# Retention scores in four 64x64 tiles with an AND mask, and shorter groups of constant matmuls in the first tile

## The chip, the cores and the metric

The kernel runs on one core of one Trainium2 chip. The metric is the time of one execution on the device in microseconds (us), the median of several runs. Beside the timed runs stands one profiled execution, from which all rows of the trace come.

## The reference

Three layers follow each other: a retention layer over q, k, v, a two-matrix MLP with a normalization ahead of it, and a mixture of four attention experts. The change touches the first alone:

```python
B, H, S, D = 2, 8, 768, 64
gamma = 1.0 - 2.0 ** (-5.0 - np.arange(H))
for t in range(S):
    state = gamma * state + einsum('bhd,bhe->bhde', k[:, :, t], v[:, :, t])
    y[:, :, t] = scale * einsum('bhd,bhde->bhe', q[:, :, t], state)
...
xn = (x - mu) / sqrt(var + 1e-06) * g_ln
x = x + maximum(xn @ w_ch1, 0.0) @ w_ch2
```

Written over chunks of tokens, a token's result is the sum of a product with the state of the chunks before and of masked scores inside its own chunk: a key counts only where it is not later than the query.

## The kernel before, in words

The retention runs over 12 tiles, (batch, chunk of 128 tokens), in `r_tile`. For one tile and the 8 heads, in pairs p of two heads h:

- the scaled values `vs` come from POOL (L422), from the load of `vk` and a small table;
- PE makes the scores (L432): for each pair and head one float32 matmul of 64 rows (the head's 64 dimensions) by 128 keys over 128 queries, into the PSUM banks `PA[0]` and `PA[1]`. The two heads of a pair lie in the two halves of the partitions, so two matmuls can run side by side;
- DVE multiplies the scores with the mask `caus` of ones and zeros into `AM` (L438);
- PE adds, in PSUM, the product with the state (L451, "inter") and the masked scores with the values (L460), and updates the state from keys and values (L467);
- the result is scaled (L476), transposed on PE (L483), normalized, transposed again and split into a rounded part and a remainder, which the MLP's matmuls (L589, L608) read.

In the trace each of these float32 matmuls is two instructions, so the 8 matmuls of a tile's scores are 16 rows' worth; transpositions are one each.

The first lines of the program issue loads on SP's queue in the order kq of tile 0 in two halves (with `tabV` and `caus` behind the first), vk, tabY, ident, then the next tiles. While the first loads are on their way, PE runs matmuls of a constant tile `negs` (`spin`, L389): 4 ahead of the scores of the first half, 2 between the halves, 8 behind the second half. The value matmuls of the first tile stand behind the last of them by the key `"spun"`:

```python
spin(4, 2.0, [], ["spun"])
...
spin(*((2, 0.5), (8, 1.7))[y0], ["scored"], ["spun"])
...
PE(1.0, intra, r=[vs] + AM + (y if c else []) + (["spun"] if i == 0 else []), w=y)
```

What stands in which order on an engine is decided by a planner (`Plan`): each step carries its engine and a cost in us (the first number in `PE(1.3 / ny, ...)`, `DVE(0.69, ...)`), its reads and its writes; `issue` plays the steps through in time by these costs and takes, whenever an engine is free, the step of lowest priority number that can run. So another cost of one step can give another order of all steps behind it, on all engines. The program's order is then fixed; what waits on the chip is held by semaphores.

Of the kernel before, what the change touches and what calls it, by code (L numbers as in the profile page):

```python
# [24 lines left out]
F32 = mybir.dt.float32  # L25
# [3 lines left out]
OP = mybir.AluOpType  # L29
# [3 lines left out]
B, H, S, D = 2, 8, 768, 64  # L33
DM = H * D
FF = 4 * DM
E, HD = 4, 64
C = 128
NC = S // C
# [14 lines left out]
KB = 256  # L53
# [154 lines left out]
def region(base, size, n, space="S"):  # L208
    return [(space, base + i * size, size) for i in range(n)]
# [3 lines left out]
def retention_channel_mlp_mixture_attention(ctx: ExitStack, tc: tile.TileContext, a):  # L213
    nc = tc.nc
    pe, act, dve, pool, sp = nc.tensor, nc.scalar, nc.vector, nc.gpsimd, nc.sync
# [3 lines left out]
    cst = ctx.enter_context(tc.tile_pool(name="cst", bufs=1))  # L219
    pp = ctx.enter_context(tc.tile_pool(name="pp", bufs=1, space=PSUM))  # L220
    ident = cst.tile([128, C], F32, name="ident")
    caus = cst.tile([128, C], F32, name="caus")
    tabV = cst.tile([128, NC, H], F32, name="tabV")
    gln = cst.tile([128, NK], F32, name="gln")
    half = cst.tile([128, 1], F32, name="half")
# [3 lines left out]
    ps = pp.tile([128, 8 * 512], F32, name="ps")  # L229
# [19 lines left out]
    def typed(dt):  # L249
        def get(b, n=None):  # L250
            v = view(b)
            if v.dtype != dt:
                v = v.bitcast(dt)
            return v[:, :n] if n else v
        return get

    f32, f32r, u32 = typed(F32), typed(F32R), typed(U32)

    o_r = 0
    o_raw = o_r + 60 * KB  # L260
# [8 lines left out]
    x = o_r  # L269
    PL = {}  # L270
    for n, size, cnt in (("kq", 4, 4), ("vk", 4, 3), ("vs", 2, 2), ("am", 2, 4), ("sn", 1, 4), ("tabY", 2, 2),
                         ("xn", 2, 2), ("xc", 2, 2)):
        PL[n] = region(x, size * KB, cnt)
        x += size * cnt * KB
    assert x <= o_raw
    PL["raw"] = region(o_raw, 4 * KB, 3)
    PL["wy"] = region(o_raw + 16 * KB, 2 * KB, 2)
    PL["wx"] = region(o_raw + 20 * KB, 2 * KB, 1)
# [12 lines left out]
    x = o_h - 2 * (4 * KB + 16)  # L291
# [22 lines left out]
    def new(n):  # L314
        return Buf(PL[n], n)

    def PE(c, fn, r=(), w=(), hold=()):
        P.add({"T": c}, lambda e: fn(), r, w, lat=0.2, hold=hold)
# [4 lines left out]
    def DVE(c, fn, r=(), w=()):  # L323
        P.add({"V": c}, lambda e: fn(), r, w)
# [4 lines left out]
    def DMA(nbytes, fn, r=(), w=()):  # L329
        P.add({"D": nbytes / 320e3 + 0.05}, lambda e: fn(), r, w, lat=2.2)  # L330
# [33 lines left out]
    def r4(ap):  # L364
        return ap.rearrange("p (a t) -> p a t", a=4)

    def load(i):
        b, c = tiles[i]
        kq, vk = new("kq"), new("vk")
        n = 2 if i == 0 else 1  # L370
        for y in range(n):
            h = slice(1024 // n * y, 1024 // n * (y + 1))
            DMA(512e3 / n, lambda h=h: sp.dma_start(f32(kq)[:, h], a["kq"][b, c][:, h]), w=[(kq, y)])
            if i == 0 and y == 0:
                DMA(24e3, lambda: sp.dma_start(tabV, a["tabV"]), w=["tabV"])
                DMA(64e3, lambda: sp.dma_start(caus, a["caus"]), w=["caus"])
        DMA(512e3, lambda: sp.dma_start(f32(vk), a["vk"][b, c]), w=[vk])
        if b == 0:
            ty = TY[c] = new("tabY")
            DMA(256e3, lambda: sp.dma_start(f32(ty), a["tabY"][c]), w=[ty])  # L380
        L[i] = (kq, vk)

    DVE(0.2, lambda: dve.memset(negs, NEG), w=["negs"])
    IDLE = new("ps")

    def spin(n, c, r, w):
        def mm():
            for _ in range(n):
                pe.matmul(f32(IDLE)[:, :C], lhsT=negs, rhs=negs, start=True, stop=True)  # L389
        PE(c, mm, r=["negs"] + r, w=[IDLE] + w)  # L390

    spin(4, 2.0, [], ["spun"])
    load(0)
    DMA(64e3, lambda: sp.dma_start(ident, a["ident"]), w=["ident"])
    load(1)
    load(2)
    DMA(2e3, lambda: sp.dma_start(gln, a["gln"]), w=["gln"])
    DVE(0.1, lambda: dve.memset(half, -0.5), w=["half"])
# [15 lines left out]
    def r_tile(i):  # L414
        b, c = tiles[i]
        j, cc = divmod(c, TPB)
        kq, vk = L[i]
        pair = lambda z, p: f32(kq)[:, p // 2 * 512 + z * 256 + p % 2 * C:p // 2 * 512 + z * 256 + (p % 2 + 1) * C]
# [5 lines left out]
             r=[vk, "tabV"], w=[vs])  # L424
        PA, AM = [new("ps") for _ in range(2)], [new("am") for _ in range(2)]
        ny = 2 if i == 0 else 1
        for y0 in range(ny):
            def scores(y0=y0):
                for p in range(4 // ny * y0, 4 // ny * (y0 + 1)):
                    for h in range(2):  # L430
                        hs = slice(64 * h, 64 * h + 64)
                        pe.matmul(f32(PA[h])[:, p * C:(p + 1) * C], lhsT=pair(0, p)[hs], rhs=pair(1, p)[hs],  # L432
                                  start=True, stop=True)
            PE(1.3 / ny, scores, r=[(kq, y0)] + (["spun"] if i == 0 else []), w=PA + (["scored"] if i == 0 else []), hold=AM)
            if i == 0:
                spin(*((2, 0.5), (8, 1.7))[y0], ["scored"], ["spun"])
        for h in range(2):
            DVE(0.69, lambda h=h: dve.tensor_tensor(r4(f32(AM[h])), r4(f32(PA[h])),  # L438
                                                    caus[:, None, :].to_broadcast([128, 4, C]), OP.mult),
                r=[PA[h], "caus"], w=[AM[h]])  # L440
        st = SN.get(b)
        y = [new("ps") for _ in range(2)]
        place = lambda g, w, z: f32(y[w])[64 * g:64 * g + 64, z * C:(z + 1) * C]
# [37 lines left out]
        def tr(dst, src):  # L481
# [3 lines left out]
           r=[(xt, cc, 0), (xt, cc, 1), "ident"], w=[t1])  # L485
# [8 lines left out]
        def rstd():  # L494
# [5 lines left out]
            r=[t1, (mv, 1)], w=[xn])  # L500
# [462 lines left out]
    for i in range(NTI):  # L963
        if i + 3 < NTI:
            load(i + 3)
        for n in early.get(i, ()):
            load_piece(*pieces[n])
        r_tile(i)
        for n in early.get(i, ()):
            P.bias += 40  # L970
            split_piece(*pieces[n])
            P.bias -= 40
# [12 lines left out]
    for n, (f, b, j) in enumerate(steps):  # L985
# [16 lines left out]
        elif j == 1:  # L1002
            hs = m_h7(f, b, rest)
# [37 lines left out]
def _layouts(q, k, v, moe_g_ln, moe_w_ch1, moe_w_ch2, moe2_w_gate, moe2_wq, moe2_wk, moe2_wv, moe2_wo):  # L1041
    def chunks_t(x):
        return x.reshape(B, NP // 2, 2, 2, NC, C, D).transpose(0, 4, 3, 6, 1, 2, 5).reshape(B, NC, 128, NP // 2, 2 * C)

    def tokens(x):
        return x.reshape(B, H, NC, C, D).transpose(0, 2, 3, 1, 4).reshape(B, NC, C, DM)

    def kxn(w):
        return w.reshape(w.shape[0] // 128, 128, w.shape[1]).transpose(1, 0, 2)

    def experts(w):
        return w.transpose(1, 0, 2).reshape(DM, E * HD)

    def f64_bits(w):
        return np.ascontiguousarray(w).reshape(NFC, 128, 1024).view(np.int64)

    order = np.arange(DM).reshape(2, 2, 2, D).transpose(2, 0, 1, 3).reshape(DM)
    moe_g_ln, moe_w_ch1, moe_w_ch2 = moe_g_ln[order], moe_w_ch1[order], moe_w_ch2[:, order]
    moe2_w_gate, moe2_wq, moe2_wk, moe2_wv = moe2_w_gate[order], moe2_wq[:, order], moe2_wk[:, order], moe2_wv[:, order]
    gamma = 1.0 - 2.0 ** (-5.0 - np.arange(H, dtype=np.float64))  # L1060
    t = np.arange(S, dtype=np.float64)
    up = gamma[:, None] ** -(t + 1)
    down = gamma[:, None] ** (t + 1) / math.sqrt(D)
    r = np.arange(C)
    o = {
        "kq": np.stack([chunks_t(k), chunks_t(q)], axis=4).reshape(B, NC, 128, 2 * DM),
        "vk": np.stack([tokens(v), tokens(k)], axis=3).reshape(B, NC, C, 2 * DM),
        "tabV": up.reshape(H, NC, C).transpose(2, 1, 0).astype(np.float32),
        "tabY": np.repeat(down, D, axis=0)[order].reshape(NP, 128, NC, C).transpose(2, 1, 0, 3).reshape(NC, 128, NP * C).astype(np.float32),
        "caus": (r[:, None] <= r[None, :]).astype(np.float32),  # L1070
        "future": (r[:, None] < r[None, :]).astype(np.uint32),
        "ident": np.eye(C, dtype=np.float32),
        "before": np.broadcast_to(np.arange(E)[None, :] < np.arange(E)[:, None], (128, E, E)).astype(np.float32),
        "gln": moe_g_ln.reshape(NK, 128).T,
        "w1": f64_bits(moe_w_ch1.reshape(NK, 128, NFC, FC).transpose(2, 1, 0, 3)),
        "w2": f64_bits(moe_w_ch2.reshape(NFC, FC // 128, 128, DM).transpose(0, 2, 1, 3)),
        "wq": kxn(experts(moe2_wq)), "wk": kxn(experts(moe2_wk)),
        "wv": kxn(np.concatenate([experts(moe2_wv), moe2_w_gate], axis=1)),
        "wo": kxn(moe2_wo.reshape(E * HD, DM)),
    }  # L1080
    return {n: np.ascontiguousarray(x) for n, x in o.items()}
# [16 lines left out]
```

## Time and profile before

| | us |
|---|---|
| median of 3 runs | 453.73 (453.58 to 453.96) |
| the profiled execution | 454.83 |
| its span, first to last instruction | 453.0 |
| busy: PE, DVE, ACT, POOL | 444.2, 326.8, 224.2, 209.6 |

The profiled execution took 454.83, of which the trace shows a span of 453.0; 1.83 lie around it. Busy time of PE counts overlapping matmuls once. Where rows are merged, "x16" is 16 instructions; a start and a length of a merged row let the time from one group's start to the next be read. The retention stage fills the first 65 us, with the MLP's first matmuls in between.

### The profile page before, as it was taken

What the parts mean: (1) busy time and instruction counts of PE and PEld (TensorE: products, weight loads), DVE (VectorE), ACT (ScalarE), POOL (GpSimd) and SP (SyncE); (2) the same over time, 40 slices, a digit from 0 to 9 for tenths busy, and PEclk for the clock granted to TensorE, in tenths of its full rate; (3) what the DMA queues carried; (4) which work ended last, traced back from release to release, by engine and by line L of the source; (5) the groups of instructions that cost most, each with busy time, mean ns of one, the idle gap of its engine ahead of it and who ended that gap; (6) DMA issues with size and microseconds to landing.
All of it is one profiled execution on the core that took longest, in us unless ns stands there. A gap on an engine that the chain in (4) does not pass through costs nothing.

```text
span 453.0 us, 8497 instructions
## 1 busy us (share of the span) xinstructions
PE 444.2 (98%) x3214; PEld 417.8 (92%) x3214; DVE 326.8 (72%) x707; ACT 224.2 (49%) x469; POOL 209.6 (46%) x216
## 2 busy tenths in 40 slices
PE   8999999999999999999999999999999999999996
PEld 7778889999999999999999999999999887898775
DVE  1798786868759867876868665569558878788852
ACT  1377567164346436344354164235535666546852
POOL 1588768978989415326145064100401334133530
PEclk9999999999999999999999999999999999999999
DMA  7798924204103103113021002002231221101111
GB/s 266 283 373 311 352 69 140 94 1 140 46 1 130 56 1 117 71 46 137 5 86 55 1 1 93 2 0 95 69 72 27 63 52 47 48 1 46 49 48 46
DMA packets 14985, 40.11 MB, mean 89 GB/s; under 512 B 2272, under 2 KB 4960, under 8 KB 14944
## 3 DMA queue, kind: packets, MB, share of 16 engines
q1 hardware_dynamic: 14944, 39.57, 25.7%
q8 instruction: 25, 0.41, 0.3%
q14 instruction: 16, 0.13, 0.1%
HBM read 33.27 MB, written 3.15 MB: 80 GB/s over the span
## 4 chain that ended last, share of the span: by engine, by line
PE 86%; DVE 8%; ACT 2%; issue 2%; DMA 1%; POOL 0%; DVEq 0%; ACTq 0%
PE ps L608 28%; PE ps L669 19%; PE ps L589 7%; PE ps L753 7%; PE ps L790 4%; PE ps L917 3%; PE ps L902 3%; PE ps L941 3%; PE ps L432 2%; PE ps L483 2%; PE ps L460 2%; PE ps L860 2%; DVE sm L868 1%; PE ps L861 1%; PE ps L389 1%
## 5 line engine op out<-in xcount | busy, mean ns | idle before, releaser
L608 PE MATMUL ps<-h,w 128*128 128x384 f32 x768 | 145.6, 335 | 0.7 <-DVE xT L612 0.4
L608 PEld LDWEIGHTS ps<-h,w 128*128 128x128 f32 x768 | 134.0, 188 | 1.4 <-DVE xT L612 0.7
L612 DVE TENSOR_TENSOR xT<-xT,ps 128x384 f32<-128x384 f32 x112 | 60.2, 549 | 36.9 <-PE ps L608 36.6
L882 POOL TENSOR_SCALAR pr<-pr,sm,gate 128x384 f32<-128x384 f32 (+5 forms) x48 | 35.1, 744 | 81.7 <-DVE ps L867 28.8
L545 POOL TENSOR_TENSOR w<-wy,w 128x512 fp32r<-128x512 f32 x26 | 33.6, 1299 | 44.2 <-PE ps L608 39.7
L669 PE MATMUL ps<-t,S 128*128 128x384 f32 x216 | 43.1, 334 | 0.0
L870 ACT ACTIVATE pr<-ps,sm 128x384 f32<-128x384 f32 (+5 forms) x48 | 30.4, 635 | 18.8 <-DVE sm L868 12.3
L676 ACT ACTIVATE u<-ps 128x384 f32<-128x384 f32 x36 | 17.6, 490 | 41.4 <-PE ps L669 35.7
L669 PEld LDWEIGHTS ps<-t,S 128*128 128x128 f32 x216 | 37.9, 188 | 0.1
L589 PE MATMUL ps<-x,w 128*128 128x384 f32 x192 | 34.9, 336 | 0.4 <-ACT wx L520 0.4
L520 ACT ACTIVATE wx<-raw 128x512 f32<-128x512 f32 x32 | 21.6, 673 | 27.5 <-DVE ps L524 19.7
L589 PEld LDWEIGHTS ps<-x,w 128*128 128x128 f32 x192 | 33.2, 188 | 0.8 <-ACT wx L520 0.6
L868 DVE TENSOR_REDUCE sm<-ps 128x1 f32<-128x384 f32 (+5 forms) x48 | 30.0, 624 | 2.8
L521 POOL TENSOR_SCALAR wx<-wx 128x512 f32<-128x512 f32 x32 | 20.3, 634 | 18.5 <-ACT wx L520 17.7
L669 PE MATMUL ps<-x,w 128*128 128x384 f32 x144 | 28.8, 334 | 0.0
L684 ACT ACTIVATE h<-ps 128x384 fp32r<-128x384 f32 x36 | 17.6, 490 | 22.5 <-PE ps L608 14.4
L669 PEld LDWEIGHTS ps<-x,w 128*128 128x128 f32 x144 | 25.3, 188 | 0.0
L544 ACT ACTIVATE w<-wy 128x512 fp32r<-128x512 f32 x26 | 16.3, 628 | 16.4 <-PE ps L608 16.1
L522 DVE TENSOR_SCALAR ps<-wx 128x512 uint32<-128x512 uint32 x32 | 22.0, 686 | 2.2 <-POOL wx L521 1.8
L526 DVE SCALAR_TENSOR_TENSOR wy<-raw,ps 128x512 uint32<-128x512 uint32 x32 | 21.8, 682 | 1.9 <-POOL w L545 1.3
L902 PE MATMUL ps<-ident,pr 128*128 128x128 f32 x168 | 22.5, 276 | 0.6 <-ACT ob L334 0.4
L524 DVE SCALAR_TENSOR_TENSOR ps<-wx,ps 128x512 uint32<-128x512 uint32 x32 | 22.3, 696 | 1.1
(119 smaller groups left out, 883.6 us busy)
## 6 DMA issues: line engine op xcount, KB each, us to landing
raw<-in_w_dram SPq DMA_DIRECT2D x32, 512.0 KB, 3.5
vk<-in_vk_dram SPq DMA_DIRECT2D x12, 512.0 KB, 5.8
kq<-in_kq_dram SPq DMA_DIRECT2D x11, 512.0 KB, 5.4
qk<-qk SPq DMA_DIRECT2D x32, 96.0 KB, 2.1
out_dram<-ob SPq DMA_DIRECT2D x11, 256.0 KB, 2.0
tabY<-in_tabY_dram SPq DMA_DIRECT2D x6, 256.0 KB, 5.2
vraw<-in_wv_dram SPq DMA_DIRECT2D x1, 520.0 KB, 3.5
kq<-in_kq_dram SPq DMA_DIRECT2D x2, 256.0 KB, 2.9
```

The lines of the kernel that those rows point to most:

```text
L522: DVE(0.62, lambda: dve.tensor_scalar(u32(z), u32(x), 4, 1, op0=OP.logical_shift_left, op1=OP.logical_shift_right), r=[x], w=[z])
L524: DVE(0.7, lambda: dve.scalar_tensor_tensor(u32(z), u32(x), 0x80000000, u32(z), op0=OP.bitwise_and, op1=OP.bitwise_or), r=[x, z], w=[z])
L545: POOL(1.34, lambda: pool.tensor_tensor(f32r(l), f32(y), f32(h), OP.subtract), r=[y, h], w=[l])
L589: pe.matmul(f32(pa, TB), lhsT=wt, rhs=blk(f32r(xt[b][j]))[:, k], start=(n == 0), stop=(n == 11))
L608: pe.matmul(f32(pa, TB), lhsT=wt, rhs=t, start=(n == 0), stop=(n == 5))
L612: DVE(0.55, lambda: dve.tensor_tensor(blk(f32(xt))[:, k], blk(f32(xt))[:, k], f32(pa, TB), OP.add), r=[pa] + [(xt, cc, w) for cc in range( ...
L669: pe.matmul(f32(pa, TB), lhsT=wt, rhs=t, start=(first and n == 0), stop=(n == 5), skip_group_check=True)
L753: pe.matmul(f32(pa, TB), lhsT=mw(n, lo, k, p * 128, (p + 1) * 128), rhs=blk(f32r(xt))[:, k], start=(i == 0), stop=(i == 11))
L868: dve.tensor_reduce(f32(sm)[:, z:z + 1], halves(f32(s), 512), axis=mybir.AxisListType.XY, op=OP.max, negate=True)
L870: ACT(act_c(nk) + .18, lambda s=s, pr=pr, z=z: act.activation(halves(f32(pr), wide), halves(f32(s), 512), AF.Exp, bias=f32(sm)[:, z:z + 1] ...
L882: POOL(0.28 + nk * 0.95e-3, lambda pr=pr, z=z, e=e: pool.tensor_scalar(f32(pr, nk), f32(pr, nk), f32(sm)[:, 6 + z:7 + z], GT[b, j][:, cc, ...
L902: pe.transpose(f32(pa)[:, i * C:(i + 1) * C], f32(PRS[z][x])[:, j * C:(j + 1) * C], ident)
```

## The change

The scores of a pair are made in four pieces of 64x64 array places (two heads by two halves m of the output partitions) instead of two. The keys of the first half of a chunk (t0 = 0) see 128 queries, those of the second half (t0 = 64) only the last 64: the quarter of the square that the mask clears is not computed. For every second pair the two halves of the keys change places in the output partitions, so that a long piece of one pair follows a short piece of the other on the same place; the host rolls `v`, `k` (as the state update reads them) and `tabV` of those heads to match. What is not written holds whatever the PSUM bank held, so the mask is now an AND with all ones or zeros (`CAUS`, twice as wide, 128 KB instead of 64), and seven of the eight banks are cleared once at the start by memsets on DVE. The constant groups have 4, 1 and 2 matmuls instead of 4, 2 and 8. The planner's costs of the scores and of the constant groups change with them.

```diff
-    caus = cst.tile([128, C], F32, name="caus")
...
+    PL["caus"] = region(x, KB, 1)
...
+    CAUS = new("caus")
...
-                DMA(64e3, lambda: sp.dma_start(caus, a["caus"]), w=["caus"])
+                DMA(128e3, lambda: sp.dma_start(u32(CAUS), a["caus"]), w=[CAUS])
...
     DVE(0.2, lambda: dve.memset(negs, NEG), w=["negs"])
+    for z in range(7, 0, -1):
+        DVE(0.55, lambda z=z: dve.memset(ps[:, 512 * z:512 * (z + 1)], 0.0))
...
-                for p in range(4 // ny * y0, 4 // ny * (y0 + 1)):
-                    for h in range(2):
-                        hs = slice(64 * h, 64 * h + 64)
-                        pe.matmul(f32(PA[h])[:, p * C:(p + 1) * C], lhsT=pair(0, p)[hs], rhs=pair(1, p)[hs],
-                                  start=True, stop=True)
-            PE(1.3 / ny, scores, r=[(kq, y0)] + (["spun"] if i == 0 else []), w=PA + (["scored"] if i == 0 else []), hold=AM)
+                for p in range(4 // ny * y0, 4 // ny * (y0 + 1), 2):
+                    for p, m, t0 in ((p, 0, 0), (p, 1, 64), (p + 1, 1, 0), (p + 1, 0, 64)):
+                        for h in range(2):
+                            hs = slice(64 * h, 64 * h + 64)
+                            pe.matmul(f32(PA[h])[64 * m:64 * m + 64, p * C + t0:(p + 1) * C],
+                                      lhsT=pair(0, p)[hs, t0:t0 + 64], rhs=pair(1, p)[hs, t0:],
+                                      start=True, stop=True, skip_group_check=True)
+            PE(1.0 / ny, scores, r=[(kq, y0)] + (["spun"] if i == 0 else []), w=PA + (["scored"] if i == 0 else []), hold=AM)
             if i == 0:
-                spin(*((2, 0.5), (8, 1.7))[y0], ["scored"], ["spun"])
+                spin(*((1, 0.3), (2, 0.6))[y0], ["scored"], ["spun"])
         for h in range(2):
-            DVE(0.69, lambda h=h: dve.tensor_tensor(r4(f32(AM[h])), r4(f32(PA[h])),
-                                                    caus[:, None, :].to_broadcast([128, 4, C]), OP.mult),
-                r=[PA[h], "caus"], w=[AM[h]])
+            DVE(0.69, lambda h=h: dve.tensor_tensor(
+                u32(AM[h]).rearrange("p (a t) -> p a t", a=2), u32(PA[h]).rearrange("p (a t) -> p a t", a=2),
+                u32(CAUS)[:, None, :].to_broadcast([128, 2, 2 * C]), OP.bitwise_and),
+                r=[PA[h], CAUS], w=[AM[h]])
```

Lines move by the added text: L389, L432, L451, L460, L467, L483 and L589 of before are L393, L437, L458, L467, L474, L490 and L596 of the change.

PE's first rows before, from the constant group to the first state update (negs is the constant tile, kq_77 tile 0's keys and queries, 4 of a row are 8 instructions of the trace):

```order
L389 MATMUL ps<-negs 128x128 x4
L432 MATMUL ps<-kq_77 128x128 x4
L389 MATMUL ps<-negs 128x128 x2
L432 MATMUL ps<-kq_77 128x128 x4
L389 MATMUL ps<-negs 128x128 x8
L460 MATMUL ps<-am_112,vs_116 64x128 x4
L460 MATMUL ps<-am_114,vs_116 64x128 x4
L467 MATMUL ps<-vs_116,vk_87 64x64 x8
```

The same place of PE in the change, up to the second value group:

```order
L393 MATMUL ps<-negs 128x128
L437 MATMUL ps<-kq_76 64x128 x2
L437 MATMUL ps<-kq_76 64x64 x2
L437 MATMUL ps<-kq_76 64x128 x2
L437 MATMUL ps<-kq_76 64x64 x2
L393 MATMUL ps<-negs 128x128 x2
L467 MATMUL ps<-am_120,vs_124 64x128 x4
L467 MATMUL ps<-am_122,vs_124 64x128 x4
L474 MATMUL ps<-vs_124,vk_90 64x64 x8
```

The order of the groups is the same here; the second constant group has one matmul, the third two, and the scores are eight smaller matmuls in place of four.

Further down, PE's rows ahead of the first group of the MLP (L589) before:

```order
L483 MATMUL ps<-ident,xn_509 128x128 x4
L483 MATMUL ps<-ident,xT_222 128x128 x4
L460 MATMUL ps<-am_480,vs_497 64x128 x4
L460 MATMUL ps<-am_494,vs_497 64x128 x4
L467 MATMUL ps<-vs_497,vk_419 64x64 x8
L432 MATMUL ps<-kq_507 128x128 x8
L451 MATMUL ps<-kq_507,sn_190 64x128 x8
L589 MATMUL ps<-x_237,w_53_381 128x384
```

And in the change, rows of the same stage of the program, some tiles behind the start:

```order
L474 MATMUL ps<-vs_495,vk_414 64x64 x8
L458 MATMUL ps<-kq_428,sn_165 64x128 x8
L490 MATMUL ps<-ident,xT_246 128x128 x4
L474 MATMUL ps<-vs_524,vk_459 64x64 x8
L467 MATMUL ps<-am_526,vs_524 64x128 x4
L467 MATMUL ps<-am_574,vs_524 64x128 x4
L490 MATMUL ps<-ident,xn_592 128x128 x4
```

The groups of different tiles alternate in another way than before: two transpositions that stood beside each other are apart, and state updates stand ahead of the values of their tile.

## Rows read from the trace of the kernel before

**Rows 1.** The page: busy time of PE, its granted clock by slices, the chain.

```profile
PE 444.2 (98%) x3214; PEld 417.8 (92%) x3214; DVE 326.8 (72%) x707; ACT 224.2 (49%) x469; POOL 209.6 (46%) x216
...
PEclk9999999999999999999999999999999999999999
...
PE 86%; DVE 8%; ACT 2%; issue 2%; DMA 1%; POOL 0%; DVEq 0%; ACTq 0%
```

**Rows 2.** Timeline of PE, 0 to 30 us: start, length, line, operands, idle before.

```profile
1.04 2.08 PE L389 MATMUL ps<-negs 128*128 128x128 f32 x8 [1.04 <-DVE half L398]
3.47 1.23 PE L432 MATMUL ps<-kq 64*128 64x128 f32 x8 [0.35 <-DMA kq<-in_kq_dram]
4.63 1.22 PE L389 MATMUL ps<-negs 128*128 128x128 f32 x4
5.78 1.23 PE L432 MATMUL ps<-kq 64*128 64x128 f32 x8
6.94 3.78 PE L389 MATMUL ps<-negs 128*128 128x128 f32 x16
10.65 1.12 PE L460 MATMUL ps<-am,vs 128*64 128x128 f32 x16
11.60 0.63 PE L467 MATMUL ps<-vs,vk 128*64 128x64 f32 x16
12.16 1.16 PE L432 MATMUL ps<-kq 64*128 64x128 f32 x16
13.25 0.66 PE L483 MATMUL ps<-ident,xT 128*128 128x128 f32 x4
...
18.11 1.09 PE L460 MATMUL ps<-am,vs 128*64 128x128 f32 x16
19.13 0.66 PE L483 MATMUL ps<-ident,xT 128*128 128x128 f32 x4
...
22.01 0.67 PE L451 MATMUL ps<-kq,sn 64*64 64x128 f32 x16
22.61 0.69 PE L467 MATMUL ps<-vs,vk 128*64 128x64 f32 x16
23.34 0.65 PE L483 MATMUL ps<-ident,xn 128*128 128x128 f32 x4
```

**Rows 3.** Timeline of all engines, 0 to 16 us: DVE, POOL and SP's queue.

```profile
0.82 0.17 DVE L383 MEMSET negs<- 128x128 f32 x1 [0.82 <-PEq L1089]
0.93 0.06 DVE L398 MEMSET half<- 128x1 f32 x1
...
7.04 1.29 DVE L438 TENSOR_TENSOR am<-ps,caus 128x512 f32<-128x512 f32 x2 [6.05 <-PE ps L432]
...
7.26 1.04 POOL L422 TENSOR_TENSOR vs<-vk,tabV 128x512 f32<-128x512 f32 x1 [6.83 <-DMA vk<-in_vk_dram]
...
12.32 0.33 SPq L377 DMA_DIRECT2D vk<-in_vk_dram  x1
```

**Rows 4.** Stretches: busy time of each engine, granted clock, DMA share, GB/s.

```profile
5.00:7.00 2.00, 2.00 (x13) 1.55 (x12) 0.00 (x0) 0.00 (x0) 0.00 (x0) 1.00 0.93 305
...
9.00:11.00 2.00, 2.00 (x15) 1.77 (x15) 0.00 (x0) 0.00 (x0) 0.00 (x0) 1.00 0.96 389
...
20.00:30.00 10.00, 9.43 (x160) 7.78 (x156) 9.29 (x19) 7.41 (x14) 7.97 (x12) 1.00 0.99 387
...
450.00:453.00 3.00, 0.00 (x0) 0.00 (x0) 0.00 (x0) 0.00 (x0) 0.00 (x0) 0.68 0.43 150
```

**Rows 5.** Groups by shape, 0 to 62 us: busy, mean ns, idle before.

```profile
L438 DVE TENSOR_TENSOR am<-ps,caus 128x512 f32<-128x512 f32 x23 | 15.1, 684 | 8.4 <-PE ps L432 8.4
...
L524 DVE SCALAR_TENSOR_TENSOR ps<-wx,ps 128x512 uint32<-128x512 uint32 x5 | 3.5, 696 | 0.2
```

**Rows 6.** The chain that ended last, 40 to 46 us.

```profile
41.04 2.35 PE ps L589 x12
```

More of the change, by code (lines that the diff above doesn't have):

```diff
@@ L274, in retention_channel_mlp_mixture_attention @@
         x += size * cnt * KB
-    assert x <= o_raw
+    PL["caus"] = region(x, KB, 1)
+    assert x + KB <= o_raw
     PL["raw"] = region(o_raw, 4 * KB, 3)
@@ L1043, in chunks_t, with turned @@
         return x.reshape(B, NP // 2, 2, 2, NC, C, D).transpose(0, 4, 3, 6, 1, 2, 5).reshape(B, NC, 128, NP // 2, 2 * C)
+    def turned(x, token, head):
+        x = x.copy()
+        y = np.moveaxis(x, (token, head), (0, 1))
+        for h in range(H):
+            if h // 2 % 2:
+                y[:, h] = np.roll(y[:, h], C // 2, axis=0)
+        return x
     def tokens(x):
-        return x.reshape(B, H, NC, C, D).transpose(0, 2, 3, 1, 4).reshape(B, NC, C, DM)
+        return turned(x.reshape(B, H, NC, C, D).transpose(0, 2, 3, 1, 4), 2, 3).reshape(B, NC, C, DM)
     def kxn(w):
@@ L1067, in _layouts @@
         "vk": np.stack([tokens(v), tokens(k)], axis=3).reshape(B, NC, C, 2 * DM),
-        "tabV": up.reshape(H, NC, C).transpose(2, 1, 0).astype(np.float32),
+        "tabV": turned(up.reshape(H, NC, C).transpose(2, 1, 0), 0, 2).astype(np.float32),
         "tabY": np.repeat(down, D, axis=0)[order].reshape(NP, 128, NC, C).transpose(2, 1, 0, 3).reshape(NC, 128, NP * C).astype(np.float32),
-        "caus": (r[:, None] <= r[None, :]).astype(np.float32),
+        "caus": np.concatenate([np.where(s[:, None] <= r[None, :], 0xFFFFFFFF, 0) for s in (r, np.roll(r, C // 2))], axis=1).astype(np.uint32),
         "future": (r[:, None] < r[None, :]).astype(np.uint32),
```

## The prediction

> **What bounds the kernel now.** I read the page first: PE is busy for 98% of the span and carries 86% of the chain that ended last [rows 1]. From 65 us on the kernel is one long row of matmuls that the change doesn't touch, so what the change saves or costs in PE's time before that should come out at the end nearly in full.
>
> Then the timeline of PE over the first 30 us [rows 2]. Its column of starts prices each kind of group, since a group's price is the distance to the next group's start. Two things are to be seen. First, the retention tiles are short groups: scores (L432) from 12.16 to 13.25, 1.09; values (L460) from 18.11 to 19.13, 1.02, but 0.95 (10.65 to 11.60) where L467 of the same array shape follows; inter (L451) from 22.01 to 22.61, 0.60; L467 from 22.61 to 23.34, 0.73 with a wait in it, and 0.56 from 11.60 to 12.16. Second, everything before 10.65 runs at half pace: 8 instructions of L432 take 1.16 from start to start at 3.47, 16 of them take 1.09 at 12.16. The view of stretches prints a granted clock of 1.00 at 9 to 11 us [rows 4]; I trust the durations, and read 1.2 GHz until about 10.7 and 2.4 GHz behind. What PE did just before the clock rose was the third group of constant matmuls, 16 instructions back to back from 6.94 to 10.65. The groups before it, which alternate with scores, had not raised it.
>
> Then the timeline of all engines at the start [rows 3], for what the first value group waited for. The mask of tile 0 is done at 7.04 + 1.29 = 8.33, the scaled values at 7.26 + 1.04 = 8.30. PE starts the value group only at 10.65 [rows 2]: some 2.3 us it works on constants alone. SP's load of the third vk at 12.32 stands behind the first L467.
>
> **The change, part by part.** All sums are made against the profiled execution (454.83, span 453.0); the median of the runs shown is 453.73, and I add the difference to that.
>
> *Start (a).* The third constant group falls from 8 matmuls to 2, the second from 2 to 1. The value group then waits for the scaled values: 8.30, plus the extra 64 KB of mask ahead of vk in the queue, at 305 GB/s [rows 4] 0.2 us, so about 8.55. Against 10.65 that is **-2.1**. The bound on the other side is no gain, when what follows waits anyway. The seven memsets: 128 columns take 0.17 and 1 column 0.06 [rows 3], so 512 take about 0.5, all seven 3.5. The first constant matmul waits for one of them: it starts at about 1.55 instead of 1.04 and its group ends near 3.65 instead of 3.12, so the first scores start 0.2 later than 3.47. They end in time: with the shorter groups the second scores end near 6.4, the masks near 7.8, still ahead of the values at 8.55. That cover hides the memsets; without it they would cost 0.5.
>
> *Scores (b).* A tile's group goes from 16 instructions of 128 columns, two abreast, to 16 of 128 and 16 of 64 on 64x64 pieces. The nearest row is L451: 64x64 pieces, 16 instructions, 0.60. From L460 (two abreast, 8 steps, 1.02) and L451 (four abreast, 4 steps, 0.60) a step is 0.105 and a group's entry and exit 0.18; L467, 8 half steps, gives 0.60 by this, between its 0.56 and 0.73. Packed without holes the new group is 6 steps: 0.81. If a short piece held its neighbours as long as a long one it would be 8 steps, 1.02. If instructions can't start closer on average than L451's (0.60 - 0.18)/16 = 0.026, it is 32 x 0.026 + 0.18 = 1.02 as well; at L451's 0.60/16 each, 1.20. I take 0.85, nearer to the packed case, since L451 shows four such pieces abreast. Times 11 groups behind the first tile: 11 x (1.09 - 0.85) = **-2.6**, with ends -3.1 and +1.2.
>
> The Trainium skill ("TensorE: Matmul & The Clock Gate", Part 1) says that starts never come closer than about 25 ns however short the matmul. By that a group would be 32 x 0.025 + 0.18 = 0.98 and this term -1.2; L451's row, at 26 ns a start on average, does not contradict it.
>
> *Order (c).* The planner gets other costs, and the order of PE from the first tile on is a new one: from the start to the last transposition of the retention stage PE runs 72 groups of one line before, 79 after. A change of group costs up to the 0.18 of entry and exit, less where the shapes agree (0.95 against 1.02); three more neighbours than before agree in shape (scores beside inter, L460 beside L467). 4 x 0.13 = **+0.5**. Waits inside the stage I leave at what they are; PE idles 0.57 us in 20 to 30 us, where DVE is busy 9.29 of 10 [rows 4]. The ends are 1 us less and 1.5 us more.
>
> *Mask (d).* A product of float32 becomes an AND of uint32 over the same 512 columns: 684 ns now, 696 ns for the kernel's own uint32 operations on PSUM [rows 5]. Taken at **0**, hidden in DVE's slack; without the slack 24 x 12 ns = 0.3.
>
> *Clock (e).* The shorter constant groups leave PE idle from about 7.5 to 8.55, and what follows are short groups with gaps, not constants back to back. Behind 8.55, each us at 1.2 GHz does half a us of work. Before, the rise came at the end of the group that starts at 6.94. In the change PE's unbroken work begins at 8.55; as far behind that as now, the rise would come at 12.3; I take 13, since the groups leave gaps. Cost (13 - 8.55)/2 = **+2.2**. No row shows whether retention groups alone raise the clock; the ends are a rise at 10.7 as now (+1.1) and one that waits for the first long groups (below).
>
> Sum: -2.1 - 2.6 + 0.5 + 0 + 2.2 = -2.0, so 451.7; I say **452.0**, with 0.3 for waits that a quicker PE meets on DVE.
>
> **The rivals.**
>
> *The clock stays low (slower).* Place: behind 8.55, in the retention tiles. Terms (a) to (c) give 4.2, so a rise at 8.55 + 2 x 4.2 = 17 decides: later than that, the kernel is slower. For it: groups with gaps at 3.47 to 6.94 did not raise the clock [rows 2], and the retention tiles are such groups. Against it: those were cut by constants of another array shape every 1.15 us, and the retention tiles follow each other with less between. At a rise at 30 us the price is 10.7 - 4.2, so 460.2. The extreme is that only the first L589 group, twelve long matmuls at 41.04 [rows 6], raises it: 30.4 us of work behind the first value group would take nearly twice as long, 453.7 - 4.2 + 29 = 478. Chance 0.34 in all, 0.08 for more than 460.5.
>
> The Trainium skill (the same page, Part 1) states this rule: the clock is low by default, and only sustained matmul activity releases it, so a filler that is cut short speaks against the change. The trace agrees that PE starts low and that the rise came at the end of the longest unbroken group; the clock's fall behind the last matmul shows as 0.68 in the last 3 us [rows 4].
>
> *The clock rises as early as now, near 10.7.* (e) is 1.1: 450.9, and 450.4 with fully packed scores. For it: PE's first 6 us are hardly changed. Against it: the idle us before 8.55 stands just where the long constant group stood. Chance 0.16.
>
> *The scores don't get shorter.* 1.02 instead of 1.09: (b) is -0.8, 453.5 to 453.8, no change that a measurement of this kernel can tell (I take 0.2%, 0.9 us, as that limit, here and below). For it: no row shows more than one start in 26 ns on average. Against it: four abreast at 128 columns. Chance 0.12, and 0.02 for other ways to the same.
>
> **How the numbers follow.** The forecast (a rise between 11.5 and 15, shorter scores) has 0.36 and holds 450.7 to 452.8; the early rise 0.16; no gain 0.14; the low clock 0.34. Faster by over 0.2% (under 452.8) is 0.36 + 0.16 = 0.52, within it 0.14, slower 0.34. The range must reach into the low clock: 449.3 (all good ends) to 460.5 leaves out 0.04 below and 0.08 above. The forecast's own range is 450.7 to 452.8.
>
> **What would show it.** (a): the first value group (line 467 of the changed kernel) starts near 8.55 and its releaser is POOL. (b): score groups of 32 instructions, 0.80 to 0.90 from start to start at full clock; near 1.02 the packing is wrong. (c): PE's idle time in 20 to 50 us no more than about 1 us above before. (e): the first pair of equal groups of which the second takes half; if transpositions still take over 1.1 us beyond 17 us, the prediction falls on the slow side. The stretch from 65 us to the end should be unchanged but shifted; if it changed by more than 1 us, the new order of the later stages has a price that I left out.

## The result and the profile after

The changed kernel took a median of 458.68 us (456.50 to 459.96, 4 runs), the kernel before 453.85 (453.58 to 454.27, 4 runs). The ratio is 1.0100, with a 95% interval of 1.0078 to 1.0121: 1.0% slower, some 4.5 us (the two medians lie 4.8 apart). The profiled execution took 459.96, the longest of the four, with a span of 458.2 against 453.0. Where one execution of a kernel took far longer than its others (1516.58 us in e4, 487.62 in e7), the ratio leaves it out.

The page of the changed kernel, the lines that answer to [rows 1]:

```profile
PE 442.7 (97%) x3392; PEld 414.8 (91%) x3392; DVE 331.5 (72%) x715; ACT 224.5 (49%) x469; POOL 209.1 (46%) x215
...
PEclk9998999999999999999999999999999999999999
...
PE 84%; DVE 6%; DMA 4%; ACT 3%; POOL 1%; issue 1%; SPq 0%; DVEq 0%; ACTq 0%; POOLq 0%
```

PE is busy for 1.5 us less than before, in a span that is 5.2 longer. Its idle time is 15.5 us instead of 8.8. In the chain that ended last PE and DVE have each lost 2 points, and DMA's share has gone from 1% to 4%. So PE did not get more to do; it waits.

The timeline of PE in the changed kernel, the rows that answer to [rows 2]; the values are L467 here, the state update L474, the transpositions L490:

```profile
1.63 2.08 PE L393 MATMUL ps<-negs 128*128 128x128 f32 x8 [1.63 <-DVE ps L387]
...
6.08 0.92 PE L437 MATMUL ps<-kq 64*64 64x128 f32 x16 [0.80 <-DMA kq<-in_kq_dram]
6.93 1.22 PE L393 MATMUL ps<-negs 128*128 128x128 f32 x4
9.67 1.98 PE L467 MATMUL ps<-am,vs 128*64 128x128 f32 x16 [1.52 <-POOL vs L426]
...
12.43 1.56 PE L437 MATMUL ps<-kq 64*64 64x128 f32 x32
13.92 0.66 PE L490 MATMUL ps<-ident,xT 128*128 128x128 f32 x4
...
21.04 0.90 PE L437 MATMUL ps<-kq 64*64 64x128 f32 x32
21.87 0.66 PE L490 MATMUL ps<-ident,xT 128*128 128x128 f32 x4
...
34.09 1.36 PE L437 MATMUL ps<-kq 64*64 64x128 f32 x32 [1.91 <-DVE wy L533]
...
36.43 1.73 PE L467 MATMUL ps<-am,vs 128*64 128x128 f32 x16
38.09 0.66 PE L490 MATMUL ps<-ident,xn 128*128 128x128 f32 x4
```

The scaled values of the first tile, which that group at 9.67 waits for:

```profile
8.57 1.04 POOL L426 TENSOR_TENSOR vs<-vk,tabV 128x512 f32<-128x512 f32 x1 [8.14 <-DMA vk<-in_vk_dram]
```

Four things are to be seen. A score group takes 21.87 - 21.04 = 0.83 at full clock instead of 1.09. The first value group starts at 9.67, not at 8.55. TensorE runs at 1.2 GHz up to about 13.9: the scores at 12.43 take 1.49 to the next start, those at 21.04 take 0.83 (the transposition at 13.92 is at full pace). And behind a wait of 1.91 us at 34 it is back at 1.2 GHz for three groups; the granted clock reads 0.57 from 34 to 38 us.

The view of stretches shows PE's busy time between 11 and 85 us. Its columns are the length, the busy time and instructions of PE, PEld (weight loads), DVE, ACT and POOL, then the granted clock, the DMA share and GB/s. Here it is of the kernel before.

```profile
11.00:20.00 9.00, 8.78 (x146) 7.25 (x144) 5.88 (x14) 2.78 (x5) 3.91 (x5) 1.00 0.67 238
30.00:40.00 10.00, 9.79 (x164) 8.28 (x162) 8.03 (x20) 6.69 (x13) 9.35 (x12) 1.00 1.00 367
40.00:50.00 10.00, 9.62 (x144) 8.48 (x144) 9.00 (x20) 5.50 (x10) 8.88 (x12) 1.00 0.85 289
50.00:65.00 15.00, 15.00 (x201) 12.53 (x198) 12.11 (x28) 9.19 (x16) 10.84 (x15) 1.00 0.58 212
65.00:85.00 20.00, 20.00 (x122) 19.92 (x122) 15.84 (x30) 11.71 (x21) 16.41 (x16) 1.00 0.30 101
```

The same stretches of the changed kernel:

```profile
11.00:20.00 9.00, 8.49 (x160) 7.10 (x158) 5.25 (x13) 2.77 (x5) 3.25 (x5) 1.00 0.65 217
20.00:30.00 10.00, 8.98 (x196) 6.89 (x195) 8.54 (x19) 6.50 (x13) 6.61 (x10) 1.00 0.96 364
30.00:40.00 10.00, 8.09 (x142) 6.72 (x138) 7.24 (x15) 5.07 (x10) 8.38 (x11) 0.83 0.89 313
40.00:50.00 10.00, 9.48 (x183) 7.84 (x184) 9.03 (x19) 6.70 (x13) 8.35 (x11) 1.00 0.78 286
50.00:65.00 15.00, 14.54 (x215) 12.89 (x213) 10.51 (x24) 9.42 (x18) 11.83 (x14) 1.00 0.84 286
65.00:85.00 20.00, 18.87 (x169) 16.92 (x170) 17.03 (x35) 12.32 (x22) 15.03 (x19) 1.00 0.29 98
```

Length less busy time, summed from 11 to 85 us (20 to 30 of before stands in [rows 4]): PE is idle for 1.4 us before and for 5.6 in the change. Ahead of 11 us it is idle for 1.4 before and for some 4 in the change, where the memsets and the shorter constant groups leave gaps. Where it waits, by the view of PE's waits in the first 85 us of the changed kernel (us in total, number of times, longest):

```profile
PE ps L437 <- DVE wy L533: 1.9, 1, 1.9
...
PE ps L467 <- POOL vs L426: 1.5, 1, 1.5
PE ps L437 <- DMA kq<-in_kq_dram: 1.3, 3, 0.8
PE ps L596 <- POOL x L513: 0.9, 1, 0.9
PE ps L596 <- ACT xc L511: 0.7, 1, 0.7
```

The last two stand at the end of the stage, in the chain that ended last:

```profile
75.79 0.45 PE ps L490 x4
...
76.33 0.61 ACT xc L511
...
76.96 0.64 ACT x L512
...
77.67 1.28 POOL x L513
...
78.99 2.20 PE ps L596 x11
```

The result of a late tile's transposition goes through two steps on ACT and one on POOL, 2.5 us, and PE has little else to run before the MLP's group that reads it. In the order of before, a longer MLP group stands in such a place, ahead of the last transposition of the stage:

```profile
69.39 6.51 PE L589 MATMUL ps<-x,w 128*128 128x384 f32 x36
75.73 0.60 PE L483 MATMUL ps<-ident,xn 128*128 128x128 f32 x4
```

In the change the last transposition comes at 81.03:

```profile
81.03 0.60 PE L490 MATMUL ps<-ident,xn 128*128 128x128 f32 x4
```

From there to the end of the span it is 377.3 us before (453.0 - 75.73) and 377.2 in the change (458.2 - 81.03). So the whole loss arises ahead of it, in the retention stage and the MLP groups mixed into it, and comes out at the end in full.

### The profile page after: what moved, and what is told of

The parts are those of the page before. It is cut to its first block, busy times and chain, and to the rows that moved or that the text cites. A ratio compares the mean times of both kernels' runs of the same rounds, so it can differ in the third digit from the quotient of the medians.

```text
span 458.2 us, 8852 instructions
## 1 busy us (share of the span) xinstructions
PE 442.7 (97%) x3392; PEld 414.8 (91%) x3392; DVE 331.5 (72%) x715; ACT 224.5 (49%) x469; POOL 209.1 (46%) x215
## 4 chain that ended last, share of the span: by engine, by line
PE 84%; DVE 6%; DMA 4%; ACT 3%; POOL 1%; issue 1%; SPq 0%; DVEq 0%; ACTq 0%; POOLq 0%
PE ps L615 28%; PE ps L676 19%; PE ps L760 7%; PE ps L596 7%; PE ps L797 4%; PE ps L924 3%; PE ps L909 3%; PE ps L948 3%; DMA vk<-in_vk_dram 3%; PE ps L490 2%; PE ps L467 2%; PE ps L867 2%; PE ps L868 1%; DVE sm L875 1%; PE ps L437 1%; PE ps L474 1%
## 5 line engine op out<-in xcount | busy, mean ns | idle before, releaser
L596 PE MATMUL ps<-x,w 128*128 128x384 f32 x192 | 35.9, 339 | 2.1 <-POOL x L513 0.9
L596 PEld LDWEIGHTS ps<-x,w 128*128 128x128 f32 x192 | 33.2, 188 | 3.5 <-POOL x L513 1.2
L676 PE MATMUL ps<-x,w 128*128 128x384 f32 x144 | 28.8, 334 | 0.0
L692 DVE SCALAR_TENSOR_TENSOR h<-ps,h 128x384 fp32r<-128x384 f32 x36 | 19.9, 552 | 4.4 <-ACT h L691 4.4
```

The source lines that it names most:

```text
L596: pe.matmul(f32(pa, TB), lhsT=wt, rhs=blk(f32r(xt[b][j]))[:, k], start=(n == 0), stop=(n == 11))
L676: pe.matmul(f32(pa, TB), lhsT=wt, rhs=t, start=(first and n == 0), stop=(n == 5), skip_group_check=True)
```

## Experiments

Each is timed against the kernel before on the same chip. The planner's order can be kept or changed without touching the work, since its costs are numbers of their own, and only one of the change's numbers matters for it: the cost of the scores alone (1.3 to 1.0) gives the new order, whether the other costs are those of before (e5) or of the change (e1). The traces bear this out: up to 85 us the groups on PE, DVE, ACT and POOL follow each other in e1 and e5 as in the change, and in e2, e3, e4, e8 and e9 as in the kernel before. SP issues its loads in one sequence in all of these. So work, order and constants can be changed one at a time.

**e1: the change with the constant groups of before, its own order kept.**

```diff
-                spin(*((1, 0.3), (2, 0.6))[y0], ["scored"], ["spun"])
+                spin(*((2, 0.3), (8, 0.6))[y0], ["scored"], ["spun"])
```

> The changed kernel with the constant groups of before (2 and 8 matmuls), the planner's costs left as they are in the change, so that the order of every engine is that of the change. Theory clock (the short groups left TensorE at 1.2 GHz until 13.9 us and the later fall at 34.4 us follows from the thin start): the clock rises near 10.7 us and stays up, and most of the 4.8 us goes: 453 to 455. Theory order (the planner's new order makes PE wait in the retention stage, whatever the clock): still 457 to 459, with PE idle for several us between 20 and 80 us.

Measured: 457.67 us, ratio 1.0073 (1.0051 to 1.0096). In the profiled execution the clock rose at about 7.2 us (the third constant group takes 2.36 instead of 3.78) and stayed up:

```profile
6.55 2.36 PE L393 MATMUL ps<-negs 128*128 128x128 f32 x16
```

That execution took 455.82, the shortest of the six, and even so more than the median before on the same chip, 454.57, if not more than the longest, 455.83; the other five took 457.00 to 459.96. So long constants do not mend the change; they bring back at most the difference between 1.0073 and 1.0100, and those intervals overlap.

**e2: the kernel before with short constant groups.**

```diff
-                spin(*((2, 0.5), (8, 1.7))[y0], ["scored"], ["spun"])
+                spin(*((1, 0.5), (2, 1.7))[y0], ["scored"], ["spun"])
```

> The kernel of before, only with 1 and 2 constant matmuls instead of 2 and 8, order unchanged. Theory clock: the rise comes 3 us later than in before, and the time grows by 1 to 4 us, 455 to 458. Theory order: the time stays within 1 us of before or falls by up to 1, since the value group starts at 8.6 instead of 10.65.

Measured: 453.78 us, ratio 0.9993 (0.9982 to 1.0003): no difference that can be told. The first value group starts at 7.97, 2.7 us earlier than in [rows 2], at half clock; nothing of it is left at the end.

**e3 and e4: the tiles in the old order**, with long and with short constant groups.

```diff
-            PE(1.0 / ny, scores, ...
+            PE(1.3 / ny, scores, ...
...
-                spin(*((1, 0.3), (2, 0.6))[y0], ["scored"], ["spun"])
+                spin(*((2, 0.5), (8, 1.7))[y0], ["scored"], ["spun"])
...
-        DVE(0.55, lambda z=z: dve.memset(ps[:, 512 * z:512 * (z + 1)], 0.0))
+        DVE(1e-6, lambda z=z: dve.memset(ps[:, 512 * z:512 * (z + 1)], 0.0))
```

> The changed kernel with the planner's costs of before for the scores and the constant groups, none for the memsets, and 2 and 8 constant matmuls: the four tiles, the AND mask and the memsets alone, in the order of before. Both theories: faster than before by what the shorter score groups give, 11 x 0.26 = 2.8 us less up to 1 us of new waits: 451 to 452.5. If it is not faster than before, the score groups were not what PE's time hung on in this stage, a third case.

> As the one before it, with 1 and 2 constant matmuls: the whole change except for the new order. Theory clock: 1 to 4 us slower than with 2 and 8, 453 to 456. Theory order: as fast as with 2 and 8 or up to 1 us faster, 450 to 452.5.

Measured: e3 453.14 us, ratio 0.9975 (0.9957 to 0.9992); e4 454.32 us, ratio 0.9992 (0.9983 to 1.0002). In the old order the tiles make the kernel faster, by 0.25% or 1.1 us (0.4 to 2.0 by the interval), against the 2.9 us by which their groups are shorter. Short constant groups cost 0.2% here, with intervals that just overlap.

**e5: the kernel before with one planner cost changed**, nothing else.

```diff
-            PE(1.3 / ny, scores, ...
+            PE(1.0 / ny, scores, ...
```

> The kernel of before with one number changed: the planner's cost of the scores is 1.0 instead of 1.3. Work, loads and constant groups are those of before; the order of every engine becomes that of the change. Theory order (the new order by itself makes the retention stage longer): 457 to 459, 3 to 4.5 us slower than before. Rival theory, that the new order only hurts together with the four tiles, the memsets or the larger mask: within 1 us of before.

Measured: 458.63 us, ratio 1.0094 (1.0072 to 1.0117). One number, the same work, the same loads, the same constants: 4.2 us. PE's stretches in its profile:

```profile
11.00:20.00 9.00, 8.79 (x146) 7.18 (x144) 6.23 (x14) 3.16 (x6) 4.58 (x6) 1.00 0.75 287
20.00:30.00 10.00, 9.19 (x147) 7.36 (x146) 8.36 (x19) 6.95 (x12) 6.98 (x11) 1.00 0.91 355
30.00:40.00 10.00, 8.69 (x152) 7.00 (x150) 7.63 (x18) 6.06 (x12) 8.56 (x12) 1.00 0.92 315
40.00:50.00 10.00, 9.31 (x132) 7.91 (x130) 7.96 (x16) 6.26 (x11) 8.53 (x10) 1.00 0.87 295
50.00:65.00 15.00, 14.31 (x173) 12.79 (x170) 11.54 (x25) 10.19 (x19) 11.39 (x16) 1.00 0.66 232
65.00:85.00 20.00, 19.09 (x155) 17.10 (x154) 16.36 (x34) 10.54 (x19) 14.89 (x17) 1.00 0.30 106
```

Idle time from 11 to 85 us is 4.6, against 1.4 before. The page's line of PE, whose span is 456.6:

```profile
PE 444.6 (97%) x3214; PEld 416.7 (91%) x3214; DVE 327.6 (72%) x708; ACT 224.8 (49%) x469; POOL 209.1 (46%) x215
```

Against [rows 1] the span is 3.6 longer: 3.2 of it is idle time of PE (12.0 instead of 8.8), 0.4 busy time. The timeline of PE shows the waits, at the places of the changed kernel's, and the last transposition of the stage:

```profile
27.81 1.16 PE L432 MATMUL ps<-kq 64*128 64x128 f32 x16 [0.66 <-DMA kq<-in_kq_dram]
...
32.37 1.16 PE L432 MATMUL ps<-kq 64*128 64x128 f32 x16 [1.31 <-DVE wy L526]
...
63.40 2.35 PE L589 MATMUL ps<-x,w 128*128 128x384 f32 x12 [0.69 <-ACT xc L504]
...
77.42 2.20 PE L589 MATMUL ps<-x,w 128*128 128x384 f32 x11 [0.91 <-POOL x L506]
79.46 0.60 PE L483 MATMUL ps<-ident,xn 128*128 128x128 f32 x4
```

From that last transposition to the end it is 377.1 us (456.6 - 79.46), as before and in the change.

**e6 and e7: the tiles with other costs**, 0.85 and 1.1 in the line of e3's first pair, else as e3.

```diff
-            PE(1.3 / ny, scores, ...
+            PE(0.85 / ny, scores, ...
```

> The four tiles, AND mask and memsets with 2 and 8 constant matmuls and a cost of 0.85 in the planner, near the 0.83 that the trace of the change shows for a score group: a third order (78 groups on PE up to the last transposition of the stage, against 72 in the old and 79 in the change's). If a truer cost makes a better order, 451 to 453. If an order is a draw whatever the cost, anything from 452 to 459; by the count of groups alone, near the change's order, 456 to 458.

> The same with a cost of 1.1: a fourth order, with 74 groups. If the count of groups on PE tells an order's price, 452.5 to 454.5; if an order is a draw, anything from 452 to 459.

Measured: e6 453.82 us, ratio 0.9992 (0.9976 to 1.0008); e7 459.12 us, ratio 1.0105 (1.0079 to 1.0131). The order with 78 groups on PE costs 0.8 us over e3's with 72 (with intervals that overlap); the one with 74 costs at least as much as the change's with 79, which with the same constants is e1 at 1.0073. So the count of groups does not rank these four; an order's price has to be measured.

**e8: the tiles in the old order without the 64-column pieces.**

```diff
-                    for p, m, t0 in ((p, 0, 0), (p, 1, 64), (p + 1, 1, 0), (p + 1, 0, 64)):
+                    for p, m, t0 in ((p, 0, 0), (p + 1, 1, 0)):
```

> The four tiles in the old order with 2 and 8 constant matmuls, but without the 64-column pieces: the second half of the keys is left out of the scores (cleared PSUM stands there), so that a score group has 16 instructions and takes 0.60 instead of 0.83. If PE's time in the retention stage sets the end, 11 x 0.23 = 2.5 us less than with the pieces: 450 to 451. If waits on DVE, POOL and the loads have taken its place, less than 1 us of that comes through: 452 to 453.5.

Measured: 452.60 us, ratio 0.9970 (0.9953 to 0.9988), beside 0.9975 of e3. Its score groups take 0.59, from one start to the next:

```profile
21.14 0.67 PE L437 MATMUL ps<-kq 64*64 64x128 f32 x16
21.73 0.66 PE L490 MATMUL ps<-ident,xT 128*128 128x128 f32 x4
```

So 2.6 us of PE's work have gone, and the time is the same within the intervals; had all of the 2.6 come through, the ratio would be near 0.992. PE's idle time between 11 and 85 us is 5.3, against 3.1 in e3: most of what PE saves, it waits. With this order and these loads PE's work is not what sets the end. Which of DVE, POOL and the loads does, no run takes apart.

**e9: the kernel before with only the memsets and the larger mask.**

```diff
+    for z in range(7, 0, -1):
+        DVE(1e-6, lambda z=z: dve.memset(ps[:, 512 * z:512 * (z + 1)], 0.0))
...
-                DMA(64e3, lambda: sp.dma_start(caus, a["caus"]), w=["caus"])
+                DMA(128e3, lambda: sp.dma_start(f32(CAUS), a["caus"]), w=[CAUS])
```

> The kernel of before with only the start of the change: the seven memsets of PSUM and a mask load of 128 KB instead of 64 (the mask repeated, the first half used), order unchanged, 2 and 8 constant matmuls. If the constant groups cover the start, as the sum for the start had it: within 0.5 us of before. If the later landing of the first vk (7.2 to 7.9 us in the kernels with the large mask, 6.4 to 6.8 without) or the later start of PE comes through, 0.5 to 1.5 us slower, which would be hidden in the gain of the four tiles in the old order.

Measured: 453.52 us, ratio 0.9997 (0.9982 to 1.0013). The start's added work costs nothing that can be told (0.2% either way).

**e10 to e12: the tiles in the old order with the mask's load behind the first vk.** e11 has the short constant groups; e12 holds the first tile's state update behind its value group, since in e10 the planner had exchanged these two.

```diff
-                DMA(128e3, lambda: sp.dma_start(u32(CAUS), a["caus"]), w=[CAUS])
         DMA(512e3, lambda: sp.dma_start(f32(vk), a["vk"][b, c]), w=[vk])
+        if i == 0:
+            DMA(128e3, lambda: sp.dma_start(u32(CAUS), a["caus"]), w=[CAUS])
```

> The four tiles in the old order with 2 and 8 constant matmuls, and the mask's load issued behind the first vk instead of ahead of it (one pair of neighbouring groups of the first tile changes places on PE). The first vk should land near 6.6 instead of 7.2 to 7.6. If the start is covered by the constants, no change against the same kernel with the mask first: 452.5 to 453.5; if not, up to 1 us faster.

> The same with 1 and 2 constant matmuls. With vk landing earlier the first value group can start near 8.6 and not 9.4 to 9.7. Theory that the clock decides: no better than the short groups with the mask first, 454. Theory that the late vk spoiled the short groups: 452 to 453, the best of all.

> The four tiles with the mask's load behind the first vk and 2 and 8 constant matmuls, but with the first tile's state update held behind its value group, so that every engine's order is that of before. It tells apart two readings of the faster run with the mask behind vk: if the place of the mask in the queue made it faster, 451.5 to 452.2 again; if the earlier state update did (it releases the third vk load, issued at 9.2 instead of about 12), 452.8 to 453.5, as with the mask first.

Measured: e10 451.75 us, ratio 0.9947 (0.9927 to 0.9967); e11 452.19 us, 0.9951 (0.9936 to 0.9967); e12 452.49 us, 0.9955 (0.9935 to 0.9974). All three are faster than the kernel before and than the change. Against the mask ahead of vk, e10 and e12 have intervals that overlap e3's, while e11 lies clear below e4 (0.9983 to 1.0002). The timeline of all engines in e10, at its start:

```profile
7.03 1.04 POOL L428 TENSOR_TENSOR vs<-vk,tabV 128x512 f32<-128x512 f32 x1 [6.61 <-DMA vk<-in_vk_dram]
7.31 1.29 DVE L446 TENSOR_TENSOR am<-ps,caus 128x512 uint32<-128x512 uint32 x2 [2.43 <-DMA caus<-in_caus_dram]
8.47 0.69 PE L476 MATMUL ps<-vs,vk 128*64 128x64 f32 x16
8.99 1.05 PE L469 MATMUL ps<-am,vs 128*64 128x128 f32 x16
...
9.23 0.33 SPq L379 DMA_DIRECT2D vk<-in_vk_dram  x1
```

The values are ready at 8.07 and the third vk load is issued at 9.23, where [rows 3] has 8.30 and 12.32. In these kernels short constant groups are no worse than long ones (e11 beside e10). Whether the mask's place or the exchange did more in e10 stays open: e12's ratio is nearer to e10's, but its interval ends just at e3's ratio.

## Why the prediction was wrong

**The step that failed is (c), the order**, as the prediction put it: seven more groups and three neighbours of equal shape, "4 x 0.13 = +0.5", waits "at what they are", with 1.5 us as the upper end. It is +4.2 us: e5 shows it alone with the work of before, and e1 against e3 shows it with the work of the change, 1.0073 against 0.9975, 4.4 us. What was counted is PE's own time at changes of group; what the order changed is what stands ready when an engine gets there. In the profiled executions of e5 and of before, 3.2 of the 3.6 us between the spans are PE's idle time. The clock rose earlier in that execution of e5 (its third constant group takes 2.95 us instead of 3.78), so at the same clock the spans would lie some 4.4 apart, an estimate; what is not idle time in that I did not take apart. Of the single waits the trace names three kinds: a weight's three steps on DVE ahead of the scores that follow them on PE (both take a PSUM bank from one pool); loads of kq that land late (behind the first tile 0.66 us in e5, 0.26 and 0.25 in the change, none before); and the last tiles' steps on ACT and POOL with nothing long beside them on PE. That these, and not others, are the price was read from the trace and not tested one by one.

**(b), the scores:** the size of a group was right, 0.83 against 0.85; the groups packed nearly without holes, and the rival by which starts could not come closer than 26 ns on average is out: in the group at 21.04 of the change the last of the 32 starts 0.67 us behind the first, 21 ns apart on average. The Trainium skill's rule ("TensorE: Matmul & The Clock Gate", Part 1) that starts never come closer than about 25 ns is not borne out here, with four pieces abreast. That the saving comes through was wrong for the change's loads: 11 x 0.26 = 2.9 us of PE's time give 1.1 us (e3), and 2.6 us more give nothing that can be told (e8). "Should come out at the end nearly in full" holds for what PE loses or gains by the end of the stage (376.6 to 377.3 us follow in every kernel but e7), and fails for PE's work inside the stage. There PE was idle for only 1.4 of 74 us before, yet much of the work that was taken off it came back as idle time: 3.1 us in e3, 5.3 in e8. The same tiles with the mask's load behind the first vk give 2.0 (e12) to 2.4 us (e10), close to the 2.6 of the forecast; so the mask's load may have held back part of the saving in e3, but those intervals overlap e3's, and this is not shown.

**(a), the start:** the value group starts at 9.67, since vk's scaled values come at 8.57 + 1.04 = 9.61 and not at 8.5; the mask ahead of vk was put at 0.2 us by its bytes. POOL starts on these values at 6.88 to 7.26 in the three kernels with the mask of 64 KB ahead of vk, at 7.75 to 8.62 in the eight with 128 KB, and at 7.03 to 7.95 in the three with the mask behind vk; so it is more than a microsecond, and why it is more than the bytes was not taken apart. The gain was mis-sized as well: in e2 the value group starts 2.7 us earlier and the kernel gains nothing measurable. "The bound on the other side is no gain" was the case. (a) and (e) together were put at -2.1 + 2.2 = +0.1, and e2, which measures only the two together, shows -0.3 (-0.8 to +0.1). The sum was right there; neither term was measured by itself.

**(d), the mask:** right. The AND takes 1.29 us for the pair, as the product did, and e9 shows the larger mask and the memsets to be free within 0.2%.

**(e), the clock:** the rise came at 13.9, near the 13 that was taken, so the rival of a clock that stays low was wrong as a mechanism; the retention groups do raise it. The price is small: short constant groups cost 0.2% in e4 over e3, nothing in e2 and e11, and 0.3% in the change over e1, both times with intervals that overlap. The second fall, at 34 us, comes behind a wait that the new order made, but, by the mean granted clock, it is not in every execution: the change's two long ones (459.42, 459.96) have a mean granted clock of 0.996, the other two (456.50, 457.93) of 0.998 and 0.999. e5, with that wait 1.31 us long, has 0.999 or 1.0 in all six and is as slow; so the price of the order does not hang on the fall. The 458.68 lie inside the stated range by luck: the range reached that far for a low clock, and the time came there by the order.

By the runs, the sum is: order +4.2 to +4.4, tiles with mask and memsets -1.1, short constants some +1.2 in the change's order, together +4.3 to +4.5, against 4.5 measured. With 4.4 the sum must close, since the three are steps from one kernel to the next (before, e3, e1, the change); the independent check is e5's 4.2.

## What to carry to other kernels

Where a planner sets the order, its cost numbers are part of the change: compare the order first with every number put back, and time the order alone with the old work (e5 is one number). A stage in which PE is busy for 98% is not for that reason bound by PE; taking work away for a trial (e8) shows whether a saving there can come out. And a small load ahead of the first large one in a queue is worth a trial behind it, if what it feeds is needed later; here it gained clearly with short constants, together with an exchange of two groups of the first tile (e11 beside e4), and with long ones within the noise.

## What the runs showed of the hardware

Four 64x64 pieces abreast, with 128 and 64 columns mixed, take 0.83 us for 32 instructions, where two abreast took 1.09 for 16; packed without holes the prediction put them at 0.81.

The view's granted clock reads 1.00 until the first recorded change, also where durations show half pace: the stretch of 9 to 11 us reads 1.00 in [rows 4], and the 16 instructions of the third constant group take 3.78 us there, while in e1, where the rise falls into that group, they take 2.36. The rise came at very different times in kernels with the same beginning: that group takes 2.36 us in e1 and 3.78 in e3, 2.06 in e10 and 3.76 in e12, and the recorded rise is at 7.2 and 10.9 us, and at 6.5 and 10.1. The full clock can also be lost again early: in the change, PE stood still for 1.91 us and TensorE was at 1.2 GHz behind it (granted 0.57 from 34 to 38 us), 1.66 us for the value group at 36.43 against 1.02 at full clock. In e1 PE stood still for 1.65 us at the same place, and the scores behind it took 0.83, the full pace.
